# A recurrent-attention and feed-forward kernel: a rewritten head, and Strassen's seven products in the last four stage pairs

## The chip, the cores and the metric

The kernel runs on one core of one Trainium2 chip. The metric is the device time of one execution in microseconds (us), taken as the median of repeated runs.

## What is computed

The reference has two parts. A gated linear recurrence runs over 4 batches, 8 heads, 768 positions and a head dimension of 48; the result, as 3072 tokens of 384 values, goes through a feed-forward network (FFN) of width 2048.

```python
state = zeros((B, H, D, D))
for t in range(S):
    cur = einsum('bhd,bhe->bhde', u[None] * kt, vt)
    y[:, :, t] = einsum('bhd,bhde->bhe', rt, state + cur)
    state = w[None, :, :, None] * state + einsum('bhd,bhe->bhde', kt, vt)
x = y.transpose(0, 2, 1, 3).reshape(3072, 384)
h = x @ w_in
out = maximum(0.01 * h, h) @ w_out
```

## The kernel before, in words

The 768 positions of a batch are cut into 6 chunks of 128. A chunk of one batch, with all 8 heads, is a **stage**: 24 stages, numbered 0 to 23. Two neighbouring stages are a **pair** m (12 pairs, 256 tokens), since the first FFN product is made for 256 tokens at once.

One letter stands for each step of a stage n:

- P (lines 305 and 307, VectorE, "DVE" in the profile): r and k are multiplied by tables of powers of w. From stage 8 on, a DMA transpose on the queue of SyncE (SP, line 310) turns the result; before stage 8, T does it with TensorE (PE, line 355), and ScalarE (ACT, line 366) copies it out of PSUM.
- A (line 377, PE): the 128x128 score blocks of the 8 heads. M (lines 387 and 391, DVE): two instructions that apply the triangular mask, one for each half of the heads.
- X (line 317), Q (lines 325 to 342) and K (lines 404 to 413): the diagonal term with u, and the sum of k and v outer products. From stage 8 on, GpSimd (POOL, line 342) writes the diagonal term into the score tile before M.
- S (lines 458 to 463, DVE): the new state. Y (line 493, PE): the output of the recurrence in transposed form; ACT copies it to xT (line 508).
- G (line 521: one stage, a quarter of the FFN width) and J (line 538: one pair, an eighth of the width): the first FFN product; ACT applies the leaky ReLU (lines 526 and 544).
- H (line 555): the second FFN product of one stage, 16 matmuls of 128x128 weights (the activations gT) by 384 columns of w_out; ACT copies it (line 561) and SP stores it (line 563).

**The order is written out by hand.** Every engine runs its own instructions in program order, and semaphores carry the dependences between engines. For the first stages (the **head**) the string ORDER (lines 26 to 31) gives the order of all steps, and LOADS (line 25) the order of the loads, which are all issued first on POOL's queue: line 210 for r, k, v; line 220 for the four quarters of w_in (wi0 to wi3); line 224 for those of w_out (wo0 to wo3). L8 to L13 load the stages 8 to 13. From pair 3 on a loop (lines 576 to 604) runs: J of pair m, Q of the stages 2m+4 and 2m+5, loads of 2m+8 and 2m+9, A and M of 2m+4 and 2m+5, Y of 2m+2 and 2m+3, K and S, P, and H of the two stages of pair m-1. The last two H stand behind the loop.

**Start.** w comes in as one row (line 230); PE spreads it over 128 partitions by a matmul with ones (line 287); ACT makes the logarithm and the two tables (lines 289 to 291). POOL makes the identity (line 255) and the mask (line 259) between the loads. DVE writes zeros into the padding of v (line 278) and of the tiles qk (line 282).

**PSUM.** Eight banks are handed out in turn by `next_bank`; a step that writes a bank waits until the reader of its last content is done.

Of the kernel before, what the change touches and what calls it, by code (L numbers as in the profile page):

```python
# [13 lines left out]
MID = 64  # L14
# [9 lines left out]
FIRST, EARLY = 6, 2  # L24
LOADS = """r1 k1 r2 k2 wi0 id v1 r3 tri k3 v2 wi1 k4 r4 v3 wi2 k5 r5 r6 k6 v4 v5 k7 wi3 r7 v6 v7 wo3 wo2 wo1 wo0"""
ORDER = """
C W P0 P1 F1 T0 T1 P2 A0 X0 M0 A1 K0 T2 Q0 X1 Y0 A2 S0 M1 K1 X2 G0.0 Q1 P3 S1 Y1 T3 K2 M2 G1.0 X3 A3 U G0.1 S2 G1.1 Q2 M3 Y2 K3 P4
T4 Q3 G2.0 G2.1 G0.2 S3 G2.2 G1.2 Y3 P5 A4 P6 X4 M4 T5 X5 G3.0 K4 Q4 A5 S4 T6 G3.1 K5 G3.2 Y4 M5 L8 Q5 Y5 P7 A6 G1.3 J2.0 J2.1 T7
M6 X6 X7 K6 J2.2 J2.3 A7 S6 J2.4 J2.5 L9 Q6 G2.3 G0.3 J2.6 M7 L10 J2.7 L11 G3.3 K7 S7 P8 Q7 Q8 P9 H0 Q9 K8 H1 P10 L12 K9 H2 S8 S9
Y6 Y7 A8 A9 P11 M8 H3 M9 L13  # L30
# [90 lines left out]
def bass_rwkv5_eagle__then__act_leaky_relu_kernel(  # L121
# [16 lines left out]
    NQK, NTP, NVS, NAT, NT, NX, NG, NO = 6, 6, 6, 6, 6, 3, 3, 4  # L138
    TURNED, DIAG = 8, 8
    w_in_sb = SB("w_in_sb", [128, NSL, DFF])  # L140
    w_out_sb = SB("w_out_sb", [128, NFB, HD])
    r_sb = SB("r_sb", [128, NST, HD])
    k_sb = SB("k_sb", [128, NST, HD])
    v_sb = SB("v_sb", [128, NST, H * E])
    w_row = SB("w_row", [1, HD], FP32)
    u_row = SB("u_row", [1, HD], FP32)
    one_row = SB("one_row", [1, 128], FP32)
# [6 lines left out]
    qtab = SB("qtab", [128, HD])  # L154
    ktab = SB("ktab", [128, HD])
    tcol = SB("tcol", [128, 1], FP32)
# [3 lines left out]
    wu_row = SB("wu_row", [1, HD])  # L160
    u_row16 = SB("u_row16", [1, HD])
    one_row16 = SB("one_row16", [1, 128])
# [7 lines left out]
    qk = [SB(f"qk{i}", [128, 2 * H, E]) for i in range(NQK)]  # L170
# [6 lines left out]
    gT = [SB(f"gT{i}", [128, NFB, 256]) for i in range(NG)]  # L177
    out_sb = [SB(f"out_sb{i}", [128, HD], FP32) for i in range(NO)]
    ps = [ctx.enter_context(nc.psum_tensor(f"ps{i}", [128, 512], FP32)) for i in range(8)]
# [22 lines left out]
    def load_one(n, which, pace=()):  # L202
        b, c = divmod(n, NC)
        t0 = c * L
        src = {"k": k, "r": r, "v": v}[which][b].rearrange("h t d -> t h d")[t0:t0 + L, :, :]
        if which == "v":
            dst = v_sb[:, n, :].rearrange("p (h e) -> p h e", e=E)[:, :, 0:D]
        else:
            dst = {"k": k_sb, "r": r_sb}[which][:, n, :].rearrange("p (h d) -> p h d", d=D)
        add("pool", lambda: G.dma_start(dst, src), R=pace, W=[(which, n)], dma=f"{which}{n}")  # L210

# [15 lines left out]
    def row(h):  # L227
        return dram(h, 0, [[HD, 1], [1, HD]])

    add("sp", lambda: SP.dma_start(w_row[:, :], row(w)), W=["w_row"], dma="w")  # L230
    add("act", lambda: A.dma_start(u_row[:, :], row(u)), W=["u_row"], dma="u")
# [3 lines left out]
    add("pool", lambda: G.iota(tcol[:, :], pattern=[[0, 1]], base=0, channel_multiplier=1,  # L235
                               allow_small_or_imprecise_dtypes=True), W=["tcol"])
    load_one(0, "v")
    add("dve", lambda: V.memset(one_row[:, :], 1.0), W=["one_row"])
    add("dve", lambda: V.memset(ones[:, :], 1.0), W=["ones"])
    add("dve", lambda: V.memset(one_row16[:, :], 1.0), W=["one_row16"])  # L240
# [11 lines left out]
    ps_w, key_w = next_bank()  # L252

    def identity():
        add("pool", lambda: G.affine_select(ident[:, :], ones[:, 0:128], pattern=[[1, 128]], compare_op=ALU.is_equal,
                                            fill=0.0, base=0, channel_multiplier=-1), R=["ones"], W=["ident"])

    def triangle():
        add("pool", lambda: G.affine_select(mask[:, :], ones[:, 0:128], pattern=[[1, 128]], compare_op=ALU.is_ge,
                                            fill=0.0, base=-1, channel_multiplier=-1), R=["ones"], W=["mask"])  # L260

    for name in LOADS.split():
        if name == "id":
            identity()
        elif name == "tri":
            triangle()
        elif name[:2] == "wi":
            load_win(int(name[2:]))
        elif name[:2] == "wo":
            load_wout(int(name[2:]))  # L270
        else:
            load_one(int(name[1:]), name[0])

    add("dve", lambda: V.tensor_scalar(kexp[:, :], tcol[:, :], -1.0, float(MID - 1), ALU.mult, ALU.add),
        R=["tcol"], W=["kexp"])
    add("dve", lambda: V.tensor_scalar(qexp[:, :], tcol[:, :], 1.0, float(-MID), ALU.mult, ALU.add),
        R=["tcol"], W=["qexp"])
    add("dve", lambda: V.memset(v_sb[:, :, :].rearrange("p n (h e) -> p (n h) e", e=E)[:, :, D:E], 0.0), W=["v0"])
    add("dve", lambda: V.tensor_tensor(wu_row[:, :], w_row[:, :], u_row[:, :], ALU.mult),
        R=["w_row", "u_row"], W=["wu_row"])  # L280
    for i in range(NQK):
        add("dve", lambda i=i: V.memset(qk[i][:, :, D:E], 0.0), W=[("qk0", i)])
    add("dve", lambda: V.memset(wl[:, :, :], 0.0), W=["wl"])
    add("dve", lambda: V.memset(wu[:, :, :], 0.0), W=["wu"])
    add("act", lambda: A.activation(u_row16[:, :], u_row[:, :], AF.Copy), R=["u_row"], W=["u_row16"])
    fill(EARLY)
    add("pe", lambda: PE.matmul(ps_w[:, 0:HD], one_row[:, :], w_row[:, :], start=True, stop=True),
        R=["one_row", "w_row"], W=[key_w, "bc"])
    add("act", lambda: A.activation(lnw[:, :], ps_w[:, 0:HD], AF.Ln), R=[key_w], W=["lnw"])
    add("act", lambda: A.activation(qtab[:, :], lnw[:, :], AF.Exp, scale=qexp[:, 0:1]), R=["lnw", "qexp"], W=["qtab"])  # L290
    add("act", lambda: A.activation(ktab[:, :], lnw[:, :], AF.Exp, scale=kexp[:, 0:1]), R=["lnw", "kexp"], W=["ktab"])
# [5 lines left out]
    def k_of(n):  # L297
        return k_sb[:, n, :] if n else k0_f[:, :]

    def r_of(n):  # L300
        return r_sb[:, n, :] if n else r0_f[:, :]

    def prep(n):
        iq = n % NQK
        add("dve", lambda: V.tensor_tensor(qk[iq][:, 0:H, 0:D], hd(r_of(n)), hd(qtab[:, :]), ALU.mult),
            R=[("r", n), "qtab", ("qk0", iq)], W=[("qp", iq)])
        add("dve", lambda: V.tensor_tensor(qk[iq][:, H:2 * H, 0:D], hd(k_of(n)), hd(ktab[:, :]), ALU.mult),  # L307
            R=[("k", n), "ktab", ("qk0", iq)], W=[("kp", iq)])
        if n >= TURNED:
            add("sp", lambda: SP.dma_start_transpose(tp[n % NTP][:, :, :],  # L310
                                                     qk[iq][:, :, :].rearrange("p h e -> p (h e)")),
                R=[("kp", iq), ("qp", iq), ("qk0", iq)], W=[("tp", n % NTP, 0), ("tp", n % NTP, 1)],
                dma=f"tp{n % NTP}")

    def diag(n):
        it, i2 = n % NTP, n % 4
        add("dve", lambda: V.tensor_tensor(prod[i2][:, :, :], tp[it][:, 0:NP, :], tp[it][:, NP:2 * NP, :], ALU.mult),
            R=[("tp", it, 0), ("tp", it, 1)], W=[("prod", i2)])

    def prep2(n):  # L320
# [8 lines left out]
        else:  # L329
            add("dve", lambda: V.tensor_tensor(ku[i2][:, :], k_of(n), u_tab[:, :], ALU.mult),  # L330
                R=[("k", n), "u_tab"], W=[("ku", i2)])
            add("dve", lambda: V.tensor_tensor(rku[i2][:, :], r_of(n), ku[i2][:, :], ALU.mult),  # L332
                R=[("r", n), ("ku", i2)], W=[("rku", i2)])
# [13 lines left out]
    def turn(n):  # L347
        it, iq = n % NTP, n % NQK
        for half in ((0, 1) if n == 0 else (1, 0)):
# [12 lines left out]
            if n == 0 and half == 1:  # L362
                add("dve", lambda dst=dst, ps_t=ps_t: V.tensor_copy(dst, ps_t[:, :]),
                    R=[key], W=[("tp", it, half)])
            else:
                add("act", lambda dst=dst, ps_t=ps_t: A.activation(dst, ps_t[:, :], AF.Copy),  # L366
                    R=[key], W=[("tp", it, half)])

    def a_mm(n):
        it = n % NTP  # L370
        at_bank[n] = (next_bank(), next_bank())
# [11 lines left out]
    def a_mask(n):  # L383
        for hh in range(2):
            part = at_bank[n][hh][0][:, :].rearrange("p (m i) -> p m i", i=128)
            if n < DIAG:
                add("dve", lambda hh=hh, part=part: V.tensor_tensor(  # L387
                    at[n % NAT][:, hh, :, :], part, mask[:, :].unsqueeze(1).to_broadcast([128, NP, 128]), ALU.mult),
                    R=[at_bank[n][hh][1], "mask"], W=[("at", n % NAT, hh)])
            else:  # L390
                add("dve", lambda hh=hh, part=part: V.copy_predicated(  # L391
                    at[n % NAT][:, hh, :, :],
                    mask[:, :].bitcast(mybir.dt.uint16).unsqueeze(1).to_broadcast([128, NP, 128]), part),
                    R=[at_bank[n][hh][1], "mask", ("at", n % NAT, hh)], W=[("at", n % NAT, hh)])
# [28 lines left out]

    def decay_columns():
        ps_c, key_c = next_bank()

        def emit():
            for hh in range(2):
                for p in range(NP):
                    c0 = (2 * p + hh) * D  # L430
# [145 lines left out]
    for m in range(FIRST // 2, NST // 2):  # L576
# [3 lines left out]
        for n in ahead:  # L580
            prep2(n)
# [82 lines left out]
```

## Time and profile before

| | |
|---|---|
| median of 3 runs | 173.33 us (173.15 to 173.61) |
| profiled execution: first to last instruction (span) | 171.8 us |
| its own time outside the span | not listed; the median of the runs is 173.33 - 171.8 = 1.5 us above this span |
| PE busy | 163.4 us (95%) |
| DVE, ACT, POOL busy | 95.7, 92.5, 102.7 us |
| DMA of POOL's queue | 76512 packets, 10.03 MB |
| HBM read, written | 20.45 MB, 4.72 MB |

The profile is of one execution. Its page gives busy time by engine, a strip of 40 slices, the chain of work that ended last, and groups of instructions by line and shape. Matmuls overlap in the array, so a group's mean duration is longer than the distance from one matmul to the next; the chain of waits, where overlapping work is merged, shows that distance.

### The profile page before, as it was taken

What the parts mean: (1) busy time and instruction counts of PE and PEld (TensorE: products, weight loads), DVE (VectorE), ACT (ScalarE), POOL (GpSimd) and SP (SyncE); (2) the same over time, 40 slices, a digit from 0 to 9 for tenths busy, and PEclk for the clock granted to TensorE, in tenths of its full rate; (3) what the DMA queues carried; (4) which work ended last, traced back from release to release, by engine and by line L of the source; (5) the groups of instructions that cost most, each with busy time, mean ns of one, the idle gap of its engine ahead of it and who ended that gap; (6) DMA issues with size and microseconds to landing.
All of it is one profiled execution on the core that took longest, in us unless ns stands there. A gap on an engine that the chain in (4) does not pass through costs nothing.

```text
span 171.8 us, 5029 instructions
## 1 busy us (share of the span) xinstructions
PE 163.4 (95%) x2179; PEld 122.4 (71%) x2179; DVE 95.7 (56%) x209; ACT 92.5 (54%) x169; POOL 102.7 (60%) x117
## 2 busy tenths in 40 slices
PE   6799999969999989999999999999999999999993
PEld 1578799859666856876877867868868768678661
DVE  7699859550999679079189197296396520000000
ACT  4755698759123841942934934825817718539121
POOL 7999999990379998972993997957207200000000
PEclk9999999999999999999999999999999999999999
DMA  5999999999999999999499499899008011011112
GB/s 98 119 150 157 171 153 173 200 179 144 112 98 240 94 145 126 202 101 116 133 93 138 128 89 143 147 116 217 0 4 214 4 46 46 4 46 50 46 48 92
DMA packets 98970, 19.66 MB, mean 114 GB/s; under 512 B 92290, under 2 KB 98948, under 8 KB 98948
## 3 DMA queue, kind: packets, MB, share of 16 engines
q0 software_dynamic: 76512, 10.03, 89.7%
q1 hardware_dynamic: 21394, 9.11, 27.1%
q8 instruction: 17, 0.28, 0.7%
q10 hardware_dynamic: 1042, 0.20, 0.6%
q14 instruction: 5, 0.04, 0.1%
HBM read 20.45 MB, written 4.72 MB: 146 GB/s over the span
## 4 chain that ended last, share of the span: by engine, by line
PE 76%; DMA 9%; DVE 6%; POOL 6%; issue 2%; ACT 0%; POOLq 0%; ACTq 0%
PE ps L555 30%; PE ps L538 28%; PE ps L521 6%; PE ps L493 6%; DMA tp<-qk 5%; DMA w_in_sb<-in_moe_w_in_dram 4%; PE ps L377 3%; PE ps L408 2%; DVE qk L307 2%; POOL v_sb L210 2%; POOL r_sb L210 2%; POOL k_sb L210 2%; PE ps L355 1%; DVE ku L330 1%; DVE s_tok L334 1%
## 5 line engine op out<-in xcount | busy, mean ns | idle before, releaser
L555 PE MATMUL ps<-w_out_sb,gT 128*128 128x384 bf16 x384 | 64.5, 326 | 0.0
L538 PE MATMUL ps<-xT,w_in_sb 128*128 128x256 bf16 x480 | 54.5, 273 | 0.0
L555 PEld LDWEIGHTS ps<-w_out_sb,gT 128*128 128x128 bf16 x384 | 36.9, 98 | 23.4
L342 POOL TENSOR_TENSOR at<-ident,s_tok 128x512 bf16<-128x512 bf16 x32 | 33.8, 1081 | 30.3 <-DVE s_tok L334 30.3
L544 ACT ACTIVATE gT<-ps 128x512 bf16<-128x512 f32 x80 | 47.8, 597 | 7.0 <-PE ps L538 2.1
L538 PEld LDWEIGHTS ps<-xT,w_in_sb 128*128 128x128 bf16 x480 | 46.7, 98 | 6.4
L561 ACT ACTIVATE out_sb<-ps 128x384 f32<-128x384 f32 x24 | 11.8, 490 | 55.1 <-PE ps L555 55.1
L391 DVE CAST_PREDICATED at<-mask,ps 128x512 bf16<-128x512 uint16 x32 | 19.8, 684 | 27.6 <-PE ps L377 25.3
L210 POOL DMA_DIRECT2D v_sb<-in_v_dram x24 | 22.6, 948 | 0.4 <-issue 0.4
L210 POOL DMA_DIRECT2D k_sb<-in_k_dram x23 | 21.7, 945 | 0.0
L210 POOL DMA_DIRECT2D r_sb<-in_r_dram x23 | 21.4, 932 | 0.0
L508 ACT ACTIVATE xT<-ps 128x384 bf16<-128x384 f32 x24 | 11.0, 490 | 4.8 <-PE ps L493 4.3
L521 PE MATMUL ps<-xT,w_in_sb 128*128 128x128 bf16 x192 | 12.3, 219 | 0.3 <-DMA w_in_sb<-in_moe_w_in_dram 0.3
L493 PE MATMUL ps<-at,v_sb 128*32 128x128 bf16 x384 | 11.9, 224 | 0.0
L521 PEld LDWEIGHTS ps<-xT,w_in_sb 128*128 128x128 bf16 x192 | 11.1, 98 | 1.0 <-DMA w_in_sb<-in_moe_w_in_dram 0.6
L526 ACT ACTIVATE gT<-ps 128x512 bf16<-128x512 f32 x16 | 9.6, 599 | 3.6 <-PE ps L521 3.0
L332 DVE TENSOR_TENSOR rku<-r_sb,ku 128x384 bf16<-128x384 bf16 x16 | 10.8, 674 | 0.5
L387 DVE TENSOR_TENSOR at<-ps,mask 128x512 bf16<-128x512 f32 x16 | 10.3, 682 | 1.3 <-PE ps L377 1.3
L493 PEld LDWEIGHTS ps<-at,v_sb 128*32 128x32 bf16 x384 | 9.1, 98 | 2.0 <-issue 0.5
L366 ACT ACTIVATE tp<-ps 128x512 bf16<-128x512 f32 x15 | 8.2, 596 | 3.8 <-PE ps L355 3.8
L493 PE MATMUL ps<-tp,st 128*32 128x128 bf16 x240 | 10.1, 219 | 0.0
L377 PE MATMUL ps<-tp 48*128 48x128 bf16 x192 | 9.1, 228 | 0.9 <-DMA tp<-qk 0.7
(62 smaller groups left out, 134.5 us busy)
## 6 DMA issues: line engine op xcount, KB each, us to landing
out_dram<-out_sb SPq DMA_DIRECT2D x24, 192.0 KB, 2.2
v_sb<-in_v_dram POOLq DMA_DIRECT2D x24, 96.0 KB, 5.9
r_sb<-in_r_dram POOLq DMA_DIRECT2D x23, 96.0 KB, 5.1
k_sb<-in_k_dram POOLq DMA_DIRECT2D x23, 96.0 KB, 5.0
w_in_sb<-in_moe_w_in_dram POOLq DMA_DIRECT2D x4, 384.0 KB, 7.4
w_out_sb<-in_moe_w_out_dram POOLq DMA_DIRECT2D x4, 384.0 KB, 11.1
tp<-qk SPq DMA_TRANSPOSE x16, 3.4
r_f<-in_r_dram SPq DMA_DIRECT2D x1, 192.0 KB, 3.5
```

Of the source, the lines that this page charges most:

```text
L210: add("pool", lambda: G.dma_start(dst, src), R=pace, W=[(which, n)], dma=f"{which}{n}")
L332: add("dve", lambda: V.tensor_tensor(rku[i2][:, :], r_of(n), ku[i2][:, :], ALU.mult), R=[("r", n), ("ku", i2)], W=[("rku", i2)])
L342: add("pool", lambda hh=hh, s_of=s_of: G.tensor_tensor(at[ia][:, hh, :, :], ident[:, :].unsqueeze(1).to_broadcast([128, NP, 128]), s_of.un ...
L377: last = PE.matmul(at_bank[n][hh][0][:, 128 * p:128 * p + 128], tp[it][rows, NP + p, :], tp[it][rows, p, :], start=True, stop=True)
L391: add("dve", lambda hh=hh, part=part: V.copy_predicated(at[n % NAT][:, hh, :, :], mask[:, :].bitcast(mybir.dt.uint16).unsqueeze(1).to_broa ...
L493: last = PE.matmul(ps_y[32 * q:32 * q + 32, 128 * s:128 * s + 128], a, m, start=first_mm, stop=last_mm)
L508: add("act", lambda: A.activation(xT[m % NX][:, :, 128 * half:128 * half + 128], ps_y[:, 0:HD].rearrange("p (s t) -> p s t", t=128), AF.Copy),
L521: last = PE.matmul(ps_g[:, 128 * f:128 * f + 128], w_in_sb[:, s, 128 * fb:128 * fb + 128], xT[ix][:, s, t], start=s == 0, stop=s == NSL - 1)
L538: last = PE.matmul(ps_g[:, 256 * f:256 * f + 256], w_in_sb[:, s, 128 * fb:128 * fb + 128], xT[ix][:, s, :], start=s == 0, stop=s == NSL - 1)
L544: add("act", lambda: A.activation(gT[ig][:, 2 * j:2 * j + 2, :].rearrange("p f t -> p (f t)"), ps_g[:, :], AF.Prelu, alpha=0.01), R=[key], ...
L555: last = PE.matmul(ps_o[:, 0:HD], gT[ig][:, s, 128 * half:128 * half + 128], w_out_sb[:, s, :], start=s == 0, stop=s == NFB - 1)
L561: add("act", lambda: A.activation(out_sb[io][:, :], ps_o[:, 0:HD], AF.Copy), R=[key], W=[("o", io)])
```

## The change

**The head.** Loads are written into ORDER itself (lower-case names), so that other POOL work can stand between them, and the order of everything is new:

```diff
-FIRST, EARLY = 6, 2
-LOADS = """r1 k1 r2 k2 wi0 id v1 r3 tri k3 v2 wi1 k4 r4 v3 wi2 k5 r5 r6 k6 v4 v5 k7 wi3 r7 v6 v7 wo3 wo2 wo1 wo0"""
+FIRST = 6
 ORDER = """
-C W P0 P1 F1 T0 T1 P2 A0 X0 M0 A1 K0 T2 Q0 X1 Y0 A2 S0 M1 K1 X2 G0.0 Q1 P3 S1 Y1 T3 K2 M2 G1.0 X3 A3 U G0.1 ...
+r1 k1 v1 Z r2 k2 P0 r4 k3 C T0 A0 X0 P1 M0.0 v2 K0 r3 W T1 Q0 k4 A1 S0 pad wi0 X1 v3 B2 M1.2 Y0 K1 T2 Q1 k5 S1 P3 X2 r5 wi3 Y1 T3 K2 v4 v5 B4 wi1 v7 k6 r6 k7 Q2 T4 S2 X3.0 r7 v6 A2 wi2 A3 F2 M2.0 M3.1 G1.0 G0.0 K3 X4.0 Q3 B5 Y2 A4 Y3 S3 T5 G2.0 M4.0 G3.0 G0.3 K4 X5.0 G1.3 wo1 wo3 wo2 Q4 wo0 K5 Q5 G3.3 S4 L8 A5 M5.0 Y4 G1.1 G2.1 G2.3 L9 G3.1 P6 Y5 T6 G0.1 X6.0 J2.7 U J2.2 B7 J2.0 T7 L10 J2.4 J2.1 K6 G0.2 Q6 G2.2 X7.1 S6 J2.5 A7 A6 M6.0 M7.1 P8 G1.2 D8 J2.6 K7 G3.2 J2.3 Y6 B9 Q7 L11 H1 Q8 S7 K8 D9 S8 H2 H3 Q9 H0 Y7 L12 A8 A9 K9 B10 D10 B11 M8 M9.0 S9 D11 L13
```

w is spread over the partitions by its own DMA (`w_bc`), and ACT reads it from there; the matmul of line 287 goes. The columns of w and w·u come from two small loads and 4 matmuls instead of 24. An `iota` of 128 columns on POOL gives a ramp, from which DVE makes identity and mask. The zero padding of the first three stages is DVE's; that of the rest is `pad`, two POOL instructions in the queue of the loads, ahead of wi0:

```diff
+        if name == "pad":
+            add("pool", lambda: G.memset(pad_v(3, NST), 0.0), W=[("v0", 1)])
+            add("pool", lambda: G.memset(qk_all[:, 3:NQK, :, D:E], 0.0), W=[("qk0", i) for i in range(3, NQK)])
```

r and k lie side by side in a ring of 16 stages, so that `prep_both` (B) does both products of P in one instruction; `turn_by_dma` (D) is the DMA transpose as a step of its own. M becomes one instruction over both halves, for which A takes two neighbouring banks; in M1.2 and M3.1 ACT copies a part out of PSUM first, and X7.1 runs on POOL. In Y of the stages 0 to 7 the twelve 32-column products with the identity become three products of 128 columns.

**The second FFN product of the pairs 8 to 11.** The pair's 256x2048 activations and the 2048x384 weights are cut into 2x2 blocks. Seven products, each 8 matmuls by 192 columns, replace the two H of the pair (32 matmuls by 384 columns). DVE makes four sums of weight blocks once (`w_sum`, 128x1536, one in each of the loop's turns m = 4 to 7) and four sums of activation blocks per pair (`g_sum`, 128x1024, in the turn m+1 between Q and M; for pair 11 at the end). Some products add up in one PSUM bank, and ACT keeps snapshots of it:

```diff
+            product(0, (0, 0), (top, one), True, False)
+            keep(0, 0)
+            product(1, 0, 0, True, False)
+            keep(1, 1)
+            product(0, 1, 1, False, False)
+            keep(0, 2)
+            product(2, (0, 1), (low, one), True, True)
+            plus(2, 0, 0, 0)
+            product(0, 2, 2, False, False)
+            plus(0, 1, 1, 1)
+            product(1, 3, (low, two), False, True)
+            plus(1, 2, 0, 1)
+            product(0, (1, 1), 3, False, True)
+            plain(0, 1, 0)
```

The first argument of `product` is the bank. `keep` is an ACT copy of 192 columns, `plus` a DVE sum of 192 columns of PSUM and a snapshot, `plain` an ACT copy to the output. A pair has 3 `keep`, 3 `plus` and 1 `plain` (instead of two ACT copies of 384 columns). Pair 11 has a variant with a fourth bank, 3 `keep`, 1 DVE sum and 4 `plus`; it ends with a `plus` and a store of half a row block.

## The prediction

> **What bounds the kernel now.** I read the page's strip first, then the chain of waits.
>
> ```profile
> PE   6799999969999989999999999999999999999993
> DMA  5999999999999999999499499899008011011112
> ```
>
> PE is full from about a third of the span on, and the DMA engines are full over the first 18 slices of 4.3 us. So there are two regions: a head in which loads arrive no faster than they are used, and a rest that is PE alone. The chain of waits, in order of time (start, us, what), puts the border at 63.24 us:
>
> ```profile
> 11.19 7.06 DMA w_in_sb<-in_moe_w_in_dram
> 18.29 1.51 PE ps L521 x24
> ...
> 26.39 0.67 PE ps L521 x12
> ...
> 34.22 1.51 issue
> ...
> 53.12 8.41 DMA tp<-qk
> ...
> 63.24 5.20 PE ps L555 x32
> 68.44 5.24 PE ps L538 x48
> ...
> 158.45 10.41 PE ps L555 x64
> 168.94 0.49 ACT out_sb L561
> ```
>
> From 63.24 on every piece starts where the last one ends: PE work taken out there is time gained. Line 555 takes 5.20/32 = 162.5 ns per 384 columns, line 538 5.24/48 = 109.2 ns per 256, line 521 0.67/12 = 56 ns per 128, each matmul with a weight load of its own. Before 63.24 three waits stand on the chain: a quarter of w_in (until 18.29), 1.5 us at 34.2, and a transpose of the stages 10 and 11 that lands at 61.5.
>
> The sum is made against the span, 171.8 us; the median of the runs is 1.5 us above it (173.33).
>
> **The head: when it can become dense.** From the chain a dense piece costs: G 0.67, a pair's eight J 5.24, H 2.60, T 0.45, A 0.33, Y 0.45 to 0.67, K 0.08 to 0.43 us. After 18.29 and up to 63.24 the kernel of before has left: 14 G (9.4), J of pairs 2 and 3 (10.5), 4 H (10.4), 5 T (2.25), 9 A (3.0), Y2 to Y9 (4.7), K2 to K10 (2.6): 42.9. 18.29 + 42.9 = 61.1; the other 2.1 us are the two waits named above.
>
> In the new order all 16 G stand behind wi0, and T0 to T4, A0 to A3, Y0, Y1 and K0 to K2 ahead of it. Left at the first G: 16 G (10.7), J (10.5), H (10.4), 3 T (1.35), 8 A (2.6), Y2 to Y9 (4.45: three products of 56 ns, 0.17 us, for twelve narrow ones worth 0.67 - 0.45 = 0.22), K3 to K10 (2.2): 42.2. So the date of **wi0** decides, and POOL's queue sets it:
>
> - The wide iota costs 0.13 (line 235, one column) to 0.57 us (line 255, a pass of POOL over 128 columns); I take 0.35, so v0 starts at 1.6 instead of 1.41 and takes 1.06. Ten loads at their distance of 0.87 (line 210) end at 11.4.
> - `pad` writes 21x128 + 3x256 = 3456 bf16 values. No row shows a long MEMSET of POOL. These rows bound it:
>
> ```profile
> L278 DVE MEMSET v_sb<- 128x1536 uint32 x1 | 1.3, 1338 | 0.3 <-issue 0.3
> L342 POOL TENSOR_TENSOR at<-ident,s_tok 128x512 bf16<-128x512 bf16 x32 | 33.8, 1081 | 30.3 <-DVE s_tok L334 30.3
> ```
>
>   At 0.83 ns per word of two values it is 1.6 us; at 2.1 ns per value, as POOL takes in a product of two inputs, 7.3. I take 1.9, near the row of the same operation. The Trainium skill, "GPSIMD Engine Reference", section 4.1, calls one-input work on GpSimd roughly line rate; an estimate of 0.83 ns for each of 3456 values would be 2.9 us, and the sum below 1.0 us more.
> - wi0 is issued at 13.3. A stage's load on an idle queue lands after 3.6 us (the one issued at 60.96), of which its 98 KB at 140 GB/s are 0.7; 393 KB at 200 GB/s are 2.0. So it lands 4.9 us later, at **18.2**.
>
> PE's work ahead of wi0 fits. The tables come about 1 us sooner, since w lands spread (192 KB, 3.5 us for r0) and PE's broadcast of 1.64 us (line 287) is gone. DVE has 13 us of work from P0 at 5.0 to M3; it ends near 19, and Y2, its first reader, comes at 20.0. Behind wi0 the loads are back to back: ten stage loads (7.0), three quarters of w_in and four of w_out (13.8) put the last quarter of w_out at 39 to 41; H1 is reached at 41.3. That slack hides the loads; a later wi0 moves both.
>
> **New wait: D10 and D11.** On SP's queue they stand behind the store of H0, which PE ends at 51.9; with ACT's copy (0.2 + 0.49) D10 is issued at 52.6, D11 at 53.9 (1.28 each, line 310), and a transpose lands 3.4 (median) to 8.4 us later (the worst, at 53.12, amid loads like here): 57.3 to 62.3. A11 is reached at 59.0. So 0 to 3.3; I take 0.8, and 0.3 for short waits. Head: 18.2 + 42.2 + 1.1 = 61.5 instead of 63.24: **-1.7**.
>
> **The seven products.** A matmul of 192 columns lies between the rows of 128 and 256: 56 + 53.2/2 = 82.6 ns. A pair takes 56 x 82.6 = 4.62 instead of 5.20 us; four pairs: **-2.3**. The Trainium skill, "TensorE: Matmul & The Clock Gate", section "Back-to-back issue gap", speaks against it: matmuls with a weight load each take about 81 ns at 128 columns and 131 at 512. An estimate between those, 89 at 192 and 114 at 384, makes seven products 1.3 us slower per pair. The trace's 56 and 162.5 ns disagree, so the sum goes by them.
>
> What it adds:
>
> - Waits on banks. Where a product adds to a bank, `keep` or `plus` must have read it, with one product (0.66) between. From a PE group to its reader are 0.2 us (68.44 + 0.655 to 69.13, and a copy's start); ACT's 192 columns are 0.33 (490 ns at 384, 597 at 512), DVE's about 0.35, from
>
> ```profile
> L461 DVE TENSOR_TENSOR sum_t<-ps,st 128x384 bf16<-128x384 f32 x11 | 6.1, 553 | 0.2
> L317 DVE TENSOR_TENSOR prod<-tp 128x512 bf16<-128x512 bf16 x8 | 3.4, 420 | 2.4 <-ACT tp L366 2.2
> ```
>
>   (1.04 ns per column). That is 0.55, so the bank is free just in time; a late semaphore shows one weight load (98 ns). Some 11 such places: 0 to 1.1 us; I take **+0.4**. ACT and DVE are otherwise idle there.
> - DVE's sums. `g_sum` is 1024 values, 0.68 us by line 317 (0.52 ns per value), `w_sum` 0.95. Those of pair 8 stand in front of the masks of the stages 22 and 23. With POOL at line 342 a DVE product took 1.08 to 1.20 instead of 0.35, so the masks start some 6 us into that turn, where A ends at 5.8; the second product needs the masked bank at 7.5. Nothing, or 0.5 us. For pair 11 they wait for the `plus` of pair 10; its second product is reached 1.3 us after that, the first sum needs 1.2 to 1.4. I take 0. w_sum runs in DVE's idle time before the mask (25.3 us in all).
> - One mask of 1.22 instead of two of 0.62: the first bank is free 1.47 us after A, the next H comes at 1.6. Nothing.
> - The tail: a DVE sum of 0.35 for a copy of 0.49: **-0.14**. The store lands in 2.2 as before; half the bytes could take 0.3 off.
>
> **Sum:** 171.8 - 1.7 - 2.3 + 0.4 - 0.1 = 168.1; with 1.5 around it **169.6 us**.
>
> **Rivals.**
>
> - *Nothing waits* (wi0 at 17.9, no wait for transposes or banks): head -3.1, products -2.3, tail -0.4: 167.5. For it: the loads' slacks above. Against: three close meetings.
> - *The products don't pay*: each of the 11 places costs 0.2 instead of 0.4 in all: +1.8, 171.4. A form of it, that every matmul waits for its own weight load (98 ns, so 5.49 us a pair instead of 5.20), would give 169.6 + 1.9 + 4 x 0.29 = 172.7; line 521 at 56 ns speaks against. That form is what the page of the Trainium skill named above comes to here.
> - *The transpose is late again*, 8.4 us as before: A11 at 62.3, 2.5 us more: 172.1.
> - *Slower:* **`pad` is slow.** It stands in front of wi0 on POOL, and all 16 G wait for it: every us beyond 1.9 is one of the head. At POOL's 2.1 ns per value it takes 7.3: 169.6 + 5.4 = 175.0. It decides from 1.9 + 3.7 = 5.6 us on. For it: the only row of POOL with hundreds of elements; against: that one reads two inputs, this one none.
>
> **How the numbers follow.** My forecast 0.50; nothing waits 0.15; products don't pay 0.15 (the form with weight loads 0.02 of it); transpose late 0.10; slow pad 0.10. Range 167.2 to 172.4: it takes in the first four, without the slow pad and the weight loads, with half a us of pad's bounds. A change of 0.3% (0.5 us) is what a measurement can tell from none: faster 0.86, within it 0.04, slower 0.10.
>
> **What would show it.** The chain's first piece of line 521 at 18.2 (later by as much as the MEMSET rows of POOL exceed 1.9); the chain dense behind it, with at most a wait for a transpose near 59; the first H of the loop at 61.5; second products of 4.6 to 4.8 us at the end instead of 5.2; no wait of PE for ACT or DVE there above 0.1. It is wrong if wi0 lands after 20, or if PE waits for g_sum.

## The result: slower by 3.7%

The changed kernel takes 179.65 us (median of 4 runs, 178.61 to 180.67) where the kernel before takes 173.47 beside it: a ratio of 1.037, 95% interval 1.0307 to 1.0433. Forecast was 169.6. The profiled execution took 180.44 us with a span of 178.6, so the gap that has to be explained is 178.6 - 168.1 = 10.5 us of span against the forecast, and 178.6 - 171.8 = 6.8 against before.

The strip of the page after, PE and the clock granted to it (40 slices of 4.5 us):

```profile
PE   0379998799999939999999999999999999999992
PEclk9999999999999985899999999999999999999999
```

Two things are new: the first three slices of PE read 0, 3 and 7 (before: 6, 7 and 9), and around slice 15 PE stands still and then runs on a lower clock. The chain of waits after (start, us, what) gives both their sizes:

```profile
19.69 1.34 PE ps_all L538 x24
...
28.14 0.58 issue
...
33.96 1.06 issue
...
58.91 7.52 DMA tp<-qk_all
...
66.57 0.61 PE ps_all L373 x8
67.18 1.62 PE ps_all L505 x52
...
69.23 6.92 PE ps_all L573 x32
76.14 5.24 PE ps_all L555 x48
...
143.63 1.22 DVE at L393
...
144.90 4.86 PE ps_all L636 x56
...
155.89 4.79 PE ps_all L636 x56
...
165.92 8.66 PE ps_all L636 x104
...
174.60 0.34 ACT snap L644
...
175.02 0.62 DVE out_sb L667 x2
```

The loop's first H, which stood at 63.24 before and was forecast at 61.5, is at 69.23, and that H takes 6.92 instead of 5.20. The second H of the loop starts at 83.28 (before: 75.57): 7.7 us are lost by then. Later the seven products give back 1.9 (4.86, 4.79 and 9.34 us for the pairs 8, 9 and 10 with 11, from the first matmul to the end of the last, where the H took 5.20, 5.31 and 10.41). Against that, 0.2 go in one turn (the H at 95.45 takes 5.37), 0.44 at 143.63 and 0.4 in the tail: 7.7 - 1.9 + 1.0 = 6.8.

What the transpose waits for is not on the chain but in SP's timeline (start, duration until the next row's work, line, what, count):

```profile
51.86 5.53 SPq L580 DMA_DIRECT2D out_dram<-out_sb  x3
57.43 16.24 SPq L294 DMA_TRANSPOSE tp<-qk_all  x4
```

Three stores, those of H2, H3 and H0, stand ahead of D10 and D11. H0 ends at 56.5, so D10 is issued at 57.43, not at 52.6, and lands 8.0 us later. PE stands still for 2.24 us ahead of A10 (until 65.59) and for 0.49 ahead of A11 (until 66.57, timeline of PE). Its granted clock falls here, in the windows' rows (window, its length, busy time of PE, PEld, DVE, ACT and POOL, then granted clock, DMA share and GB/s):

```profile
65.00:70.00 5.00, 3.93 (x80) 2.82 (x81) 3.06 (x4) 0.98 (x2) 5.00 (x7) 0.58 0.89 74
70.00:75.00 5.00, 5.00 (x24) 2.69 (x23) 4.23 (x9) 0.49 (x1) 4.24 (x5) 0.74 1.96 137
```

A clock of 0.58 over 5 us and 0.74 over 5 us is half the clock for 4.2 + 2.6 = 6.8 us. In windows of half a us it reads 1.00 until 65.5, 0.76 from 65.5 to 66.0 and 0.50 from there to 72.5: it falls some 0.2 us after A10 starts, ahead of the second, shorter wait. The short pieces behind the waits took 2.66 us (66.57 to 69.23) where the kernel before takes 1.58 (61.66 to 63.24), and the H 1.7 too long: 2.8 us on top of the 2.7 of the waits themselves.

### The profile page after: what moved, and what is told of

Read it like the earlier page. It is cut to its first block, busy times and chain, and to the rows that moved or that the text cites. A ratio compares the mean times of both kernels' runs of the same rounds, so it can differ in the third digit from the quotient of the medians.

```text
span 178.6 us, 5066 instructions
## 1 busy us (share of the span) xinstructions
PE 162.0 (91%) x2183; PEld 128.9 (72%) x2183; DVE 106.9 (60%) x195; ACT 95.3 (53%) x179; POOL 107.2 (60%) x118
## 4 chain that ended last, share of the span: by engine, by line
PE 85%; DMA 7%; issue 2%; DVE 1%; ACT 1%; DVEq 0%; SPq 0%
PE ps_all L555 26%; PE ps_all L573 24%; PE ps_all L636 10%; PE ps_all L538 6%; PE ps_all L505 6%; DMA tp<-qk_all 4%; PE ps_all L373 4%; DMA r_f<-in_r_dram 3%; PE ps_all L353 3%; PE ps_all L422 2%; PE ps_all L510 1%; ACT tp L360 1%; DVE at L393 1%; PE ps_all L427 1%; PE ps_all L418 1%
## 5 line engine op out<-in xcount | busy, mean ns | idle before, releaser
L555 PE MATMUL ps_all<-xT,w_in_sb 128*128 128x256 bf16 x480 | 54.7, 273 | 0.0
L555 PEld LDWEIGHTS ps_all<-xT,w_in_sb 128*128 128x128 bf16 x480 | 46.6, 98 | 5.9
L561 ACT ACTIVATE gT<-ps_all 128x512 bf16<-128x512 f32 x80 | 47.5, 597 | 6.0 <-PE ps_all L555 1.5
L573 PE MATMUL ps_all<-w_out_sb,gT 128*128 128x384 bf16 x256 | 44.7, 335 | 0.0
L573 PEld LDWEIGHTS ps_all<-w_out_sb,gT 128*128 128x128 bf16 x256 | 25.2, 100 | 16.9 <-issue 1.9
L393 DVE CAST_PREDICATED at<-mask,ps_all 128x1024 bf16<-128x1024 uint16 x16 | 18.8, 1219 | 28.5 <-PE ps_all L373 28.5
L212 POOL DMA_DIRECT2D rk_sb<-in_k_dram x23 | 21.8, 948 | 0.5 <-PE ps_all L555 0.5
L212 POOL DMA_DIRECT2D rk_sb<-in_r_dram x23 | 21.4, 932 | 0.0
L525 ACT ACTIVATE xT<-ps_all 128x384 bf16<-128x384 f32 x24 | 11.1, 490 | 11.1 <-PE ps_all L505 6.9
L538 PE MATMUL ps_all<-xT,w_in_sb 128*128 128x128 bf16 x192 | 12.3, 219 | 1.1 <-issue 1.1
L538 PEld LDWEIGHTS ps_all<-xT,w_in_sb 128*128 128x128 bf16 x192 | 11.1, 98 | 1.7 <-issue 1.2
L505 PE MATMUL ps_all<-at,v_sb 128*32 128x128 bf16 x384 | 12.1, 235 | 0.0
L543 ACT ACTIVATE gT<-ps_all 128x512 bf16<-128x512 f32 x16 | 9.5, 601 | 2.6 <-PE ps_all L538 2.3
```

The source lines that it names most:

```text
L212: add("pool", lambda: G.dma_start(dst, src), R=pace, W=[key], dma=f"{which}{n}")
L393: add("dve", lambda: V.copy_predicated(dst, mask[:, :].bitcast(mybir.dt.uint16).unsqueeze(1).to_broadcast([128, H, 128]), src), R=keys + [ ...
L505: last = PE.matmul(ps_y[32 * q:32 * q + 32, 128 * s:128 * s + 128], a, m, start=first_mm and (s == 0 or n >= DIAG), stop=last_mm and n >= ...
L525: add("act", lambda: A.activation(xT[m % NX][:, :, 128 * half:128 * half + 128], ps_y[:, 0:HD].rearrange("p (s t) -> p s t", t=128), AF.Copy),
L538: last = PE.matmul(ps_g[:, 128 * f:128 * f + 128], w_in_sb[:, s, 128 * fb:128 * fb + 128], xT[ix][:, s, t], start=s == 0, stop=s == NSL - 1)
L555: last = PE.matmul(ps_g[:, 256 * f:256 * f + 256], w_in_sb[:, s, 128 * fb:128 * fb + 128], xT[ix][:, s, :], start=s == 0, stop=s == NSL - 1)
```

## The experiments

Fifteen kernels, each against the kernel before on the same chip. The theory: the loss is the new head's alone, and in it the order of the queues (stores ahead of the transposes) and what follows from it on the clock. The rivals: the seven products cost time, or the head's loads do. Each ratio is to the kernel before, timed beside that kernel, and kernels are compared by their ratios; 0.01 is 1.7 us.

### Each half alone

The head of before with the new second products (`second` is g2_seven from pair 8 on, and H before):

```diff
+    SEVEN = 8
+        second(m - 1)
```

> The head of before with the seven products of the changed kernel (r and k in a ring of 15 stages, so that the new tiles fit). Theory A (the whole loss is the head's, the products gain): in the trace the pairs 8 to 11 went from 5.20 to 4.85, 4.79 and 9.17 for two, so -2.0 us, +0.4 where DVE's sums delay the mask, +0.5 at the tail: 1.1 us faster than before, 172.3. Rival C (the products cost as much as they save, by DVE's sums and the tail): within 0.5 us of before, 173.3, or slower.

Measured: 171.74, ratio 0.9917 (0.9876 to 0.9958). The changed head with H for all pairs and no sums:

```diff
-        if m >= SEVEN:
-            g2_seven(m)
-        else:
-            g2(2 * m)
+        g2(2 * m)
```

> The rewritten head with the old second product for all pairs (no sums, no seven products). Theory A: the head carries the whole loss, so about 1.1 us slower than the changed kernel: 180.7. Rival C: the products carry a part of the loss, so faster than the changed kernel, 178 or less.

Measured: 179.63, ratio 1.0413 (1.0344 to 1.0482). So the products gain about 1.4 us, and the head loses some 7. The rival that the products don't pay falls. The chain of the first of these kernels shows them without any wait:

```profile
136.33 4.69 PE ps L624 x56
141.02 5.24 PE ps L543 x48
...
147.15 4.79 PE ps L624 x56
```

The clock of the four executions of the head alone reads 1.0, 0.981, 0.99 and 0.99: in the profiled one the waits at A10 and A11 were 1.78 and 1.32 us and the clock stayed whole.

### The transposes, and the clock behind the wait

Q9, B10, D10, B11 and D11 ahead of H2, H3 and H0:

```diff
-... D9 S8 H2 H3 Q9 H0 Y7 L12 A8 A9 K9 B10 D10 B11 M8 M9.0 S9 D11 L13
+... D9 S8 Q9 B10 D10 B11 D11 H2 H3 H0 Y7 L12 A8 A9 K9 M8 M9.0 S9 L13
```

> The changed kernel with Q9, B10, D10, B11 and D11 written ahead of H2, so that SP issues the two transposes before the stores of H2, H3 and H0. Theory A (they land late because they stand behind those stores): issued near 51 and 52.5 instead of 57.4 and 58.9, landed before A10 is reached (63.3); the wait of 2.9 us, the half clock behind it (2.9 us) go: 5.8 us less, 173.9. Rival B (a transpose lands late because the DMA engines are full of loads, whenever it is issued): the loads of the stages 12 and 13 still meet it, the wait stays to at least a half: 177 or more.

Measured: 176.27, ratio 1.0173 (1.0127 to 1.022). 3.4 us come back, less than expected. The loop's first H is at 64.92 with the clock whole, but the next turn takes 14.4 us instead of 12.2, by a chain that had lain hidden behind the first wait:

```profile
62.27 4.21 POOL at L340 x4
...
66.50 1.23 DVE at L393
...
70.36 7.04 DMA tp<-qk_all
...
79.28 5.20 PE ps_all L573 x32
```

POOL's diagonal tiles of the stages 10 and 11 start only at 62.27 (before: 56.81), because the masks M8 and M9 (line 393) come behind all four H of the head, at 57.7 (before: 53.0). Behind them on DVE are the masks of 10 and 11, the prepared tiles of 12 and 13, and on SP their transposes.

The clock by itself was tried in the changed kernel by filling the wait:

```diff
+        if m == FIRST // 2:
+            fill(14)
```

> The changed kernel with 14 matmuls of 512 columns on ones (no result of theirs is used) between J of pair 3 and A of stage 10, 3.0 us of PE in the time in which it waits for the transposes. Theory A (the clock falls since PE stands still there): the granted clock stays 1.00 between 65 and 75, the pieces behind the wait take 1.4 and 5.2 us instead of 2.7 and 6.9: 2.9 us less, 176.7. Rival (the clock falls for another reason, such as the long dense stretch before): the clock still falls, and the time is 179.6 or more.

Measured: 176.83, ratio 1.0211 (1.0164 to 1.0259). The second transpose lands as long after H0 as in the changed kernel (65.30 behind 54.83, there 66.43 behind 56.50), yet the clock stays whole, the first H takes 5.20 and the time falls by 2.8 us. So the half clock is from PE's standing still, and is worth as much as the wait. (The profiled execution is faster by more than that, as two waits in the middle of the head, 0.58 and 1.06 us in the changed kernel, are 0 and 0.19 in it. From the end of H0 to the end of the loop's first H it is 17.4 us instead of 19.6.) The Trainium skill, "TensorE: Matmul & The Clock Gate", part "The HAM clock gate", says that the clock is halved after an idle window of about 3.4 us. In the changed kernel it was halved after 2.24 us of standing still; the trace decides.

### The masks

Besides the early transposes, A8, A9 and their masks ahead of H0:

```diff
-... H2 H3 H0 Y7 L12 A8 A9 K9 M8 M9.0 S9 L13
+... H2 H3 A8 A9 M8 M9.0 H0 Y7 L12 K9 S9 L13
```

> The run with the four early transposes, and besides the score products and masks of stages 8 and 9 (A8 A9 M8 M9.0) ahead of the last second product of the head (H0) instead of behind it. Theory: with the transposes in time, the next thing late is the chain on VectorE and GpSimd: masks of 8 and 9 only at 57.7 to 60.0 us, then the diagonal tiles of 10 and 11 on GpSimd at 62.3 to 66.5, the masks of 10 and 11 until 67.7, the prepared tiles of 12 and 13 at 68.5, and their transposes landing at 77.4, so that the second loop turn takes 14.4 us instead of 12.2. With the masks some 3 us sooner that turn takes 12.2 and the time falls from 176.3 to about 174.1. Rival: the transposes simply take 7 us to land under the load of the stages' inputs, and the wait stays: 176 or more.

Measured: 175.0, ratio 1.0098 (1.007 to 1.0125): 1.3 us. The second turn is 12.3 us long, the transposes do land in time, and the rival falls; but the loop's first H comes at 65.59, 0.7 later than in the run before, since Y7 now stands right ahead of the loop and its copy by ACT is waited for:

```profile
57.91 0.50 ACT xT L525
...
65.59 5.20 PE ps_all L573 x32
```

Y7 ahead of H0 was tried twice. On top of the next section's early first products:

> The same as the run with early first products, and Y of stage 7 ahead of the last second product of the head instead of behind it. Theory: the loop's first products waited some 0.8 us (57.3 to 57.8 us in the run before) for ScalarE's copy of that Y; with 2.7 us of products between, nothing waits: 0.5 to 0.8 us faster. Rival: what stood behind the wait, the diagonal tiles and masks of 10 and 11 and the transposes, becomes late by as much: within 0.2 us.

Measured: 174.29, ratio 1.0034 (1.0007 to 1.0062) against 1.0058 (1.0032 to 1.0084), unsettled by the intervals. The second time is below.

### The zero fills and the early loads

The changed kernel's groups have the two fills of `pad` (line, engine, operation, output, shape, count, then busy us, mean ns, and idle time before):

```profile
L258 POOL MEMSET v_sb<- 128x2688 bf16 x1 | 2.4, 2448 | 0.0
...
L259 POOL MEMSET qk_all<- 128x768 bf16 x1 | 0.8, 848 | 0.0
```

3.3 us in front of every later load. First only wi0 and v3 were moved past them (`S0 wi0 X1 v3 pad` for `S0 pad wi0 X1 v3`):

> The same as the run with early masks, and besides the two zero fills on GpSimd (3.3 us) behind the loads of w_in's first quarter and of v's stage 3 instead of ahead of them. Theory: these two loads set the start of the dense part (first G at 19.7 us, and a wait for v's stage 3 until 21.3); 3.3 us sooner they set it no longer, and what is left is TensorE's own chain of the first stages, so that the first G comes at 18 to 19.4 and the time falls by 1 to 2 us, to 172.1 to 173.1. Rival: TensorE's chain of the first stages ends at the same 19.5 us anyway, and later loads (v4, r5, w_in's other quarters), which stay where they were, set the rest: below 0.5 us.

Measured: 174.47, ratio 1.0067 (1.0046 to 1.0088): 0.5 us, the rival's size. The first G comes at 19.22, though wi0 is issued at 11.17 instead of 14.03. But the chain of this run goes through the moved fills themselves: the second ends at 15.84, and only then is stage 3 prepared (DVE, 15.87) and turned (PE, 16.64). So this run does not tell what an earlier wi0 is worth; the kernels at the end of this section do. On this one, the old narrow form of Y:

> The same as the run with the later zero fills, and besides the old form of the products of Y for the first eight stages: the 12 narrow matmuls of vs by the identity among the 28 others, instead of three of 128 rows behind them. Theory: the new form takes 0.50 + 0.27 = 0.77 us where the old one took 0.67 for 40, so that eight stages pay 0.1 us each, six of them in the dense part: 0.6 us faster than the run before it. Rival: the dense part waits for loads and evictions, and TensorE's 0.1 us per stage are hidden: within 0.2 us.

Measured: 175.17, ratio 1.0116 (1.0076 to 1.0155): no gain, if anything a loss. Its chain goes through a load of r (issued at 33.10, landed 11.61 later), the preparation of stage 9 and its transpose, so cheaper PE pieces changed nothing. Also on the later fills, wi0 behind k2 and two G moved ahead of the others, to 16.3 and 19.1 us, in place of the two matmuls on ones (F2):

```diff
-r1 k1 v1 Z r2 k2 P0 r4 k3 C ... Y1 T3 K2 ... Q2 T4 S2 ... A3 F2 M2.0 M3.1 G1.0 G0.0 K3
+r1 k1 v1 Z r2 k2 wi0 P0 r4 k3 C ... Y1 G0.0 T3 K2 ... Q2 T4 G1.0 S2 ... A3 M2.0 M3.1 K3
```

> The run with the later zero fills, and besides w_in's first quarter loaded right behind k's stage 2 (as the head of before has it) and the first two products of the dense part (24 matmuls of 56 ns) in TensorE's idle time between the first stages: one behind stage 1's Y, one behind stage 4's transposes, in place of the fills. Theory: the new head is dearer in its dense part because these products, which the old head did at 14 us where TensorE was idle, stand in it (192 narrow matmuls from the first one of the chain to the loop instead of 168): 24 times 56 ns is 1.3 us and the fills 0.4, so the loop begins 0.7 to 1.5 us sooner and the time falls from 174.5 to about 173.3. Rival: ScalarE evicts these products between the transposes' copies, 0.64 us each, and the early chain is longer by as much, or late loads of the stages 8 and 9 hold the loop's start: 174.2 or more.

Measured: 174.81, ratio 1.0058 (1.0032 to 1.0084): the same as without. Its chain names what is late instead, a load of k behind wi0:

```profile
10.97 7.03 DMA rk_sb<-in_k_dram
...
18.02 0.57 DVE qk_all L309
```

Three edits of PE's and two loads' order moved 0.5 us in all. What was left to try was to take the 3.3 us away from all loads, by giving the fills back to DVE, which is idle from 2.6 to 6.3 us:

```diff
-            add("pool", lambda: G.memset(pad_v(3, NST), 0.0), W=[("v0", 1)])
+    add("dve", lambda: V.memset(pad_v(3, NST), 0.0), W=[("v0", 1)])
```

(and the same for the other fill), in the changed kernel alone, then with early transposes and masks, then with Y7 ahead of H0 as well:

> The changed kernel with one part undone alone: the two zero fills are VectorE's again (where it stands idle from 2.6 to 6.0 us), not GpSimd's, so that every load behind them is issued 3.3 us sooner. Theory: the first G moves only from 19.7 to about 19, because TensorE's own chain of the first stages ends there, and the four late transposes stay behind the stores, so the time falls by 0.5 to 1.5 us: 178.2 to 179.2. Rival: the loads bind everywhere in the head, and all of the 3.3 us come back: 176.4.

> The run with early transposes and early masks, and besides the zero fills on VectorE as in the run before this one. Theory: what the order of the queues costs is gone, and now the loads show: r of stage 9 was issued at 33 us and landed at 44.8, where VectorE waited 0.5 to 0.7 us for it, and the earlier loads land late in the same way; all issued 3.3 us sooner, the time falls by 1 to 1.7 us, from 175.0 to 173.3 to 174.0. Rival: the 16 DMA engines are busy nine tenths of the time, so an earlier issue only waits longer, and the gain is that of the moved fills alone: 0.5 us, 174.5.

> The same as the run before this one, and besides Y of stage 7 ahead of the last second product of the head. Theory: the 0.5 us wait of the loop's first products for ScalarE's copy goes: 0.5 us faster, 172.8 to 173.5. Rival: the masks and transposes are late in its place: within 0.2 us.

Measured: 178.55, ratio 1.0262 (1.0208 to 1.0316), 1.9 us by the ratios; 173.98, ratio 1.0013 (0.9988 to 1.0038), 1.5 us better than with the fills on POOL; 173.65, ratio 0.9993 (0.9968 to 1.0017). Y7 is worth 0.3 us at most, inside the intervals. In the last kernel the loop's first H is at 63.86, where it is at 63.24 before.

These runs also show what else holds the first G. The first and the last of them have the same order of the early steps and issue wi0 at about 11 us, and both chains reach the first G through PE's own work on the first stages. Yet it comes at 18.61 in the first (two lines) and at 19.66 in the last (two lines):

```profile
16.07 0.57 PE ps_all L354 x8
18.61 1.34 PE ps_all L539 x24
16.42 0.85 PE ps_all L354 x8
19.66 1.34 PE ps_all L539 x24
```

The eight matmuls of a T take 0.85 us on the chain early in the span and 0.45 from some point on, though the profile lists a clock of 1.00 throughout. In the timelines of PE (matmuls of a T, 1.05 us while slow and 0.62 after) that point lies near 14 us in the kernel before, near 16 in the first of these two and near 18 in the last and in the changed kernel. So 1.05 us of the first G's date hang on when PE comes to its full rate. The old head has PE at work from 1.65 us on, with matmuls on ones and the spreading of w; in the new head PE's first matmul is at 6.5. Whether that is the reason was not tried.

### What w's DMA does to the tables

In the kernel before, w spread by a DMA in place of the matmul of line 287:

> The kernel before with one part of the new head alone: w is spread over 128 partitions by a DMA with stride 0, and the matmul that did it goes (the row is still loaded for the decay columns). Theory: the spread lands at 5.0 us where the row landed at 2.6, so the first decay tables come at about 6.0 to 6.7 instead of 5.5 to 6.0, and stage 0's first prepared tile at 7.0 instead of 6.5; the dense part begins with w_in's landing at 18.3 all the same, so that the time is within 0.5 us of before. Rival, as the prediction had it: the matmul and its wait go, the tables come 1 us sooner.

Measured: 173.99, ratio 1.0027 (1.0 to 1.0053). ACT's timeline, the logarithm of w before:

```profile
4.29 0.49 ACT L289 ACTIVATE lnw<-ps 128x384 f32<-128x384 f32 x1 [0.69 <-PE ps L287]
```

and with the spread:

```profile
4.74 0.52 ACT L289 ACTIVATE lnw<-w_bc 128x384 f32<-128x384 f32 x1 [1.13 <-DMA w_bc<-in_w_dram]
```

The tables come 0.45 us later, not 1 sooner: here the spread lands later than the row and the matmul together.

### How far the products go

With the old head, the last pair by H again, and five pairs instead of four (`SEVEN = 7`):

> The head of before with seven products in the pairs 8, 9 and 10, and the last pair with all eight (384 columns at a time) as before. Theory: the products gain 0.58 us a pair, but the last pair's three VectorE sums and half-row stores lengthen the end from 2.95 us behind the last matmul to 4.1, so that the last pair loses about 0.5 net: 171.2 against 171.7 for seven products in all four. Rival: the end is the stores' landing anyway, and without the last pair's gain it is 172.3.

> The old head with seven products in five pairs, 7 to 11, instead of four. Theory: each pair's product gets shorter by 0.5 us (4.7 instead of 5.2) as long as VectorE's sums (2.9 us for gT and 0.65 for the outputs of a pair) find room beside masks and prepared tiles: in turn 8 VectorE has about 9 of 12.2 us taken, so that they just fit, and the time falls from 171.7 to 171.2. Rival: in that turn the masks stand behind the sums and the product waits for them, as in turn 9 of the changed kernel (0.44 us): 171.6 or more.

Measured: 171.65, ratio 0.9914 (0.9885 to 0.9944), the same as four pairs; and 172.45, ratio 0.9952 (0.9925 to 0.998), no better than four and, the intervals overlapping, perhaps 0.6 us worse. The last pair's gain (9.34 us for two pairs instead of 9.90) goes into its longer end: the span ends 3.4 us behind the last matmul instead of 2.95. With five pairs, DVE's queue in turn 8 is full, from the chain of that kernel:

```profile
122.90 2.47 DVE at L396 x4
...
128.29 0.54 DVE out_sb L655 x2
...
128.88 0.83 PE ps L624 x8
```

Masks, states and prepared tiles stand ahead of the `plus` of the products (line 655), and PE's next product waits for its bank. The best kernels of the study are these with the old head: 171.7, 0.8% faster than before.

## Why the prediction was wrong, step by step

The head failed, and in it the step "D10 is issued at 52.6" with its wait of 0.8 us: D10 was issued at 57.43 and the waits were 2.7 us. By the second H of the loop the kernel is 9.4 us behind the forecast (7.7 lost where 1.7 were to be gained). H0 ended 4.6 us later than forecast, the waits for the transposes were 1.9 longer, and the half clock, which no step has, took 2.8.

- **"PE work taken out there is time gained"**, the products at 82.6 ns: right. A pair takes 4.79 to 4.86 us where 4.62 and 0.1 for banks were forecast, the last two together 9.34; in all -1.9, as forecast. The rival "the products don't pay", and its form with weight loads, fall.
- **"D10 is issued at 52.6"**: the order, D10 behind the store of H0, was read rightly, but H0 ended at 56.5, not 51.9. Of these 4.6 us 1.5 are the first G, 1.6 the waits of 0.58 and 1.06 us (next item), 0.8 that each of five Y took 0.50 + 0.27 instead of 0.62, and 0.7 are spread over small pieces. Then the transpose took 8.0 us to land, near the upper end given. The wait was 2.7 us instead of 0.8.
- **"0.3 for short waits"**: 1.6. Both stand in the middle of a group of G, where the profile names nothing that PE waits for, like the 1.51 us at 34.22 before, which the forecast took as a wait that goes. Kernels with the same order up to there have 0.2 (the fills at A10) to 2.2 us of them (the zero fills on DVE alone); their cause stays open.
- **The rival "transpose late again"** priced the wait alone. That PE's clock is halved after it was in neither forecast nor rival, and doubled the price: 2.8 us.
- **"New wait: D10 and D11"** stopped at the transposes. The same order put M8 and M9 4.7 us later, and POOL's diagonal tiles with them: 1.3 us once the first wait is gone.
- **`pad` 1.9 us**: it was 3.30. The row of DVE's MEMSET that set the value counts words of two values; POOL's rows count single values, 0.91 and 1.1 ns each. The estimate of 2.9 us by the Trainium skill, "GPSIMD Engine Reference", section 4.1, which the prediction set aside, was nearer to the 3.30 of the trace.
- **"So the date of wi0 decides"**: half right. wi0 landed at 19.35 and the first G ran at 19.69, but with wi0 issued 3.0 us sooner (fills on DVE, last kernel) it still ran at 19.66.
- **"PE's work ahead of wi0 fits"**: wrong. PE's work on the first stages bound the first G too; the forecast made no sum of it, and PE takes 0.85 us instead of 0.45 for a T in most of this time. And with 16.4 us of PE busy in the first 19.6 before, and 11.1 after, all 16 G are packed behind that point, while the old head had done two of them earlier.
- **"That slack hides the loads"**: wrong. Every load from wi0 on stood behind 3.3 us of fills, and giving that time back was worth 1.5 to 1.9 us.
- **"The tables come about 1 us sooner"**: 0.7 later in the changed kernel, 0.45 by the spread alone.
- **g_sum ahead of the masks, "nothing, or 0.5"**: 0.44. In the old head the same sums cost nothing (136.33, above); there the masks are halves and the banks others, and which of the two it is was not tried.
- **The tail, -0.14**: +0.4, three `plus` in a row and several half-row stores.

In ratios, the way back from 1.037: early transposes 1.0173, early masks 1.0098, fills on DVE 1.0013, Y7 0.9993, the old head 0.9917. What the last step is made of (0.6 us at the loop's first H, 0.4 at turn 9, the rest within the intervals) was not taken apart further; PE's late full rate may be part of it. The forecast gain of 1.7 us in the head does not exist in any of the versions tried.

## What to carry to other kernels

When a list of orders is rewritten by hand, compute for each in-order queue the moment at which its longest-waiting instruction is released, and then follow what stands behind it; a transpose behind three stores is late by the last of the three. A wait that lets PE stand still for some 2 us can cost twice, as here. Check that a repair removes the second wait that lay hidden behind the first. An engine that is idle (DVE from 2.6 us) is a better place for a fill than a queue that issues the loads.

## What was not expected of the hardware

- The clock granted to PE is halved for 6.8 us after it stands still for 2.24 us. In the head alone it stays whole through waits of 1.78 and 1.32 us within 3.5 us; with the zero fills on DVE alone it falls behind waits of 1.79 and 0.66 (that H takes 6.62). The length of the waits alone does not decide.
- PE takes nearly twice as long per T (0.85 us against 0.45) until 14 to 18 us into the span, with a listed clock of 1.00.
- A zero fill on POOL takes 0.91 ns per bf16 value (2448 ns for 2688; 848 for 768), on DVE 0.87 per pair of values (1338 ns for 1536 words).
- Three products of 128 columns by the identity behind Y take 0.27 us on the chain, not three times 56 ns.
